# One power on GpSimd for the inverse norms, and reciprocals of one column in thirty-two

## The chip, the cores and the metric

The kernel runs on one core of a Trainium2 chip. The metric is the device time of one execution in microseconds (us). A core has TensorE (PE, the products), VectorE (DVE), ScalarE (ACT), GpSimd (POOL) and queues that start transfers (DMA); the queue used for nearly all of them is that of SyncE (SP). Each engine carries out its instructions in the order in which the program lists them and waits, where needed, for others.

## The reference

The inputs `q`, `k` and `v` have 8 batches, 12 heads, 448 rows and 64 columns; all numbers are float32 on arrival.

```
rmsnorm(x, g) = x / sqrt(mean(x * x) + 1e-6) * g          # over the 64 columns
q_n, k_n = rmsnorm(q, g_q), rmsnorm(k, g_k)
scores = q_n @ k_n^T / sqrt(64)
attn = exp(scores - max) / (sum of exp over the keys + 1e-9)
x = (attn @ v), heads side by side: 3584 rows x 768 columns
out = (silu(x @ w_gate) * (x @ w_val)) @ w_out             # 768 -> 1536 -> 768
```

The two places that matter here are the inverse root of the norms (one number for each row of `q` and of `k`) and the division by the sums over the keys (one number for each query).

## The kernel before

The function `fast` does all the work; `general` is there for gains outside a range and isn't run with these inputs. The heads are handled in pairs: 48 pairs, `m = 0 .. 47`, each handled by a call of `attention(m)`. The rows of the matrices after the attention are handled in four blocks of two batches, `block(n)`. Every product with a weight matrix is made of 15 products of combined thirds (the lists `UP_ORDER` and `DOWN_ORDER`), with sums of the operands formed beforehand (`sides` for the activations, `convert` for the weights) and sums of the results afterwards (`read`).

Nothing is issued in the order in which the Python functions are called. Each step calls `order.add(engine, us, when, emit, ...)` with a planned duration `us`, a due time `when`, the steps that it follows and the buffers that it takes or uses. At the end `order.run()` walks through all steps, picks the next for each engine by planned times, and calls the `emit` functions in that order. So a new planned duration changes the order of instructions on all engines. Two modes of ACT, `logarithms` and `silu`, have their own table loads (lines L552 and L1402 of the profile); a step that names the other mode makes a load.

The profile falls into an **opening** of some 140 us, in which the first twelve pairs are prepared and weighted while the first of the 18 pieces of weights are loaded, converted and stored again in device memory, and four blocks. In a block the up products (L1328) run first, then the down products (L1502) together with the attention of twelve later pairs.

One pair goes through these steps:

- SP loads `q` and `k` into tiles named `qk`, within `work` in the profile (L728), and `v` (L744, L747).
- ACT squares both (L754); DVE adds up each run of 32 columns (L768); ACT swaps halves between partitions with four small copies (L778); DVE adds the two halves (L782). The result `ss` has 28 columns on 128 partitions.
- `inverse_root`: on ACT a logarithm (L678) and an exponential (L679) give an estimate `rr`; on DVE three instructions (L684, L685, L686) improve it by one Newton step.
- GpSimd scales `k` and `q` by `rr` (L795), DVE transposes them in 32-by-32 squares (L811), ACT scales the queries by the gains (L814).
- PE makes the scores (L840, four parts), ACT the exponentials (L855). In the opening PE adds these up over the keys (L947 with four terms); later GpSimd (L860) and DVE (L866) add most of them first.
- PE makes the weighted values (L916); ACT copies one half of the result (L1005) and DVE adds the other (L1008).
- `invert`, on DVE: the reciprocal of the sums, 224 columns (L982). The tile of sums has four strips of 32 partitions, and within a strip all 32 rows hold the same numbers, as each strip is a product with a constant matrix (`many`, `halves`).
- The reciprocals are spread to 128 partitions, in the opening by a product (L990) and later by eight copies on ACT (L1000), and DVE multiplies (L1012).

GpSimd also makes the sums of weight thirds in `convert` (L1199, L1202), ahead of which come two ACT copies (L1146, L1150) and six DVE steps (L1168, L1174, L1180). The loads of pieces that go into the places ES, PAIRS and the third of GT wait for the last sum over keys of the opening.

The rings of buffers that the change touches are `ss=2`, `rr=4`, `rd=1` (reciprocals) and the `t=2` tiles of squares and scaled values.

Of the kernel before, what the change touches and what calls it, by code (L numbers as in the profile page):

```python
# [9 lines left out]
F32 = mybir.dt.float32  # L10
U32 = mybir.dt.uint32
I64 = mybir.dt.int64
AF = mybir.ActivationFunctionType
ALU = mybir.AluOpType
# [346 lines left out]
class Order:  # L361
# [24 lines left out]
    def add(  # L386
        self, engine, us, when, emit, after=(), takes=(), uses=(), port=False, kb=0, group=None,
        mode=None, early=None, rank=0.0, slack=0.1,
    ):
        piece = dict(  # L390
            engine=engine, us=us, when=when, emit=emit, takes=takes, port=port, kb=kb,
            group=group, mode=mode, early=early, rank=rank, slack=slack,
            after=[a for a in after if a is not None], end=None, n=len(self.pieces),
        )
        for tile_of in (*takes, *uses):
            self.users.setdefault(tile_of, []).append(piece)
        self.pieces.append(piece)
        return piece
# [79 lines left out]
def fast(  # L478
# [41 lines left out]
    nc = tc.nc  # L520
    B, H, S, D = q.shape
    DM = H * D
    DFF = moe_w_gate.shape[1]
    P = 128
    NJ = 4
    Q = S // 2
# [6 lines left out]
    C = 32  # L533
# [6 lines left out]
    const = ctx.enter_context(tc.tile_pool(name="const", bufs=1))  # L540
# [3 lines left out]
    ctx.enter_context(tc.manual_schedule())  # L544

    BUFS = dict(
        qk=4, v=2, t=2, QT=2, KT=2, e=4, ea=7, eh=2, sums=1, inv=1, rd=1, rows=3, st=2, at=2, ss=2,
        rr=4, ws=2, **{x + str(i): 1 for x in "vw" for i in range(6)},
    )

# [3 lines left out]
    order = Order(BUFS, dict(logarithms=load_tables))  # L554
    tiles = {}
# [10 lines left out]
    def take(name, key, shape):  # L566
        if name in ("e", "ea"):
            at = order.turn[name] % BUFS[name]
            tiles[name, key] = es[:, at] if at < BUFS["e"] else more_es[:, at - BUFS["e"]]
            return tiles[name, key]  # L570
        if name in OFTEN:
            at = OFTEN[name] + order.turn[name] % BUFS[name]
            tiles[name, key] = spare[:, ts(at, S)]
            return tiles[name, key]
        if name == "eh":
            at = order.turn["eh"] % BUFS["eh"]
            tiles[name, key] = more[:, at].rearrange("p (h q) -> p h q", h=2)
            return tiles[name, key]
        if name in WORK:
            at, size = WORK[name]  # L580
            at += order.turn[name] % BUFS[name] * size
            n = 1
            for length in shape[1:]:
                n *= length
            x = work[0 : shape[0], at : at + n]
            letters = "abcd"[: len(shape) - 1]
            x = x.rearrange(
                f"p ({' '.join(letters)}) -> p {' '.join(letters)}",
                **dict(zip(letters, shape[1:])),
            )  # L590
            tiles[name, key] = x
            return x
        pool = psum if name in ("st", "at") else sbuf
        tiles[name, key] = pool.tile(shape, F32, name=name, bufs=BUFS[name])
        return tiles[name, key]
# [33 lines left out]
    gq2 = const.tile([P, 1], F32, name="gq2")  # L629
    gk2 = const.tile([P, 1], F32, name="gk2")  # L630
    gg = const.tile([P, 1], F32, name="gg")

# [29 lines left out]
    down_products = {}  # L664


    GAIN = 2.0**24

    SCALE = 2.0**8
    SPREAD = 6.0  # L670

    def inverse_root(m, sums, of, when, rank=0.0):


        def estimate():
            ss = of()
            rr = take("rr", m, list(ss.shape))
            nc.scalar.activation(rr, ss, AF.Ln, scale=GAIN**-2)  # L678
            nc.scalar.activation(rr, rr, AF.Exp, scale=-0.5)  # L679

        def improve():
            ss, rr = of(), tiles["rr", m]
            times = nc.vector.scalar_tensor_tensor
            times(ss, rr, GAIN**-2, ss, op0=ALU.mult, op1=ALU.mult)  # L684
            times(ss, ss, -0.5, rr, op0=ALU.mult, op1=ALU.mult)  # L685
            times(rr, ss, 1.5, rr, op0=ALU.add, op1=ALU.mult)  # L686

        first = order.add(
            "ACT", 0.5, when, estimate, after=[sums], uses=[("ss", m)], takes=[("rr", m)],
            mode="logarithms", rank=rank,  # L690
        )
        return order.add(
            "DVE", 0.45, when + 1.0, improve, after=[first], uses=[("ss", m), ("rr", m)],
            rank=rank,
        )

    NC = S // C
    clusters = {}
# [4 lines left out]
    def attention(m):  # L703
# [7 lines left out]
        b, c = batch_pair(m)  # L711
        base, span = pair_time(m)

        ready = base - span
        early = m < EARLY
        rank = 60.0 if early else 0.0
# [40 lines left out]
        for x in range(2):  # L757
# [3 lines left out]
                    after=[loaded[x], *squares], uses=[("qk", (m, x))] + [("t", m)] * x,  # L761
# [26 lines left out]
        )  # L788
        sums = add("ACT", 0.9, ready - 16.0, swap, after=[sums], uses=[("ss", m)])
        sums = add("DVE", 0.15, ready - 15.0, both, after=[sums], uses=[("ss", m)])  # L790
        rr = inverse_root(m, sums, lambda: tiles["ss", m][:, 0], ready - 14.0, rank)

        def scale(x):
            rr = tiles["rr", m][:, ts(x, NC)].rearrange("p (c one) -> p c one", one=1)
# [184 lines left out]


        def invert():
            nc.vector.reciprocal(take("rd", m, [P, Q]), tiles[den])  # L982


        def spread_place():
# [24 lines left out]
        def divide():  # L1010
# [5 lines left out]
        )  # L1016
        joined = add("DVE", 0.64, when + 4.0, join, after=[copied, last], uses=at[1:])
        inv = add(
            "DVE", 1.52, when + 4.0, invert, after=[all_sums], uses=[] if of_bank else [den],
            takes=[("rd", m)],  # L1020
        )
        if early:
            inv = add(
# [565 lines left out]


    nc.gpsimd.memset(many, SCALE)
    nc.gpsimd.memset(halves, 0.0)
    for x in range(2):
        nc.gpsimd.memset(halves[ds(D * x, D), x], SCALE)
# [7 lines left out]
    for i in range(P // C):  # L1602
# [2 lines left out]
    gains = order.add(  # L1605
        "DVE", 0.2, 9.0,
        lambda: nc.vector.scalar_tensor_tensor(
            out=gg, in0=gq2, scalar=8.0 * GAIN**-2, in1=gk2, op0=ALU.mult, op1=ALU.mult
        ),
        early=0.0,  # L1610
    )
# [21 lines left out]
@with_exitstack  # L1633
def kernel(
    ctx: ExitStack,
    tc: tile.TileContext,
    q: bass.AP,
    k: bass.AP,
    v: bass.AP,
    g_q: bass.AP,  # L1640
    g_k: bass.AP,
    moe_w_gate: bass.AP,
    moe_w_val: bass.AP,
    moe_w_out: bass.AP,
    out: bass.AP,
):


    nc = tc.nc
    args = (q, k, v, g_q, g_k, moe_w_gate, moe_w_val, moe_w_out, out)  # L1650
    D = q.shape[3]
    guard = ctx.enter_context(tc.tile_pool(name="guard", bufs=1))
    g2 = guard.tile([1, 2, D], F32, name="g2")
    gp = guard.tile([1, D], F32, name="gp")
    top = guard.tile([1, 1], F32, name="top")
    fits = guard.tile([1, 1], mybir.dt.int32, name="fits")
    for i, x in enumerate((g_q, g_k)):
        nc.scalar.dma_start(g2[:, i], x.rearrange("(one d) -> one d", one=1))
    nc.vector.tensor_tensor(out=gp, in0=g2[:, 0], in1=g2[:, 1], op=ALU.mult)
    nc.vector.tensor_reduce(  # L1660
        out=top, in_=gp, axis=AX.X, op=ALU.max, apply_absolute_value=True
    )
    nc.vector.tensor_scalar(out=fits, in0=top, scalar1=8.0, scalar2=None, op0=ALU.is_le)
    fast(tc, *args)
    fits = nc.values_load(fits[0:1, 0:1], min_val=0, max_val=1)
    with tc.If(fits == 0):
        general(tc, *args)
# [30 lines left out]
```

## Time and profile before

| what | value |
|---|---|
| median of 3 runs | 1487.9 us (1486.89 to 1488.19) |
| span of the profiled execution, first to last instruction | 1484.0 us |
| distance of the median from that span | 3.9 us |
| PE busy, mean granted clock | 1425.0 us, 0.997 |
| DVE, ACT, POOL busy | 916.0, 681.5, 414.1 us |
| PE idle ahead of its first product | 14.66 us |

The page gives no time of the profiled execution other than its span; what lies around it can only be seen as the distance from the median of the runs. A row of a group in the profile reads: line, engine, operation, output and inputs by the program's names, shapes and count, then busy time in us and the mean in ns of one instruction, then the idle time of that engine just ahead of them and what ended most of it. A row of a wait reads: the engine and group that waited, what it waited for, the total in us, how many times, and the longest.

### The profile page before, as it was taken

How to read it: one execution, taken by the hardware profiler on the slowest of the kernel's cores; microseconds unless marked ns; L12 is line 12 of the kernel's file. 1: busy time of each engine (PE TensorE's matmuls, PEld its weight loads, DVE VectorE, ACT ScalarE, POOL GpSimd, SP SyncE). 2: the span in 40 equal slices, each digit the busy share in tenths (PEclk: the TensorE clock that was granted, in tenths of full speed). 3: DMA queues.
4: the chain of work that ended last, by engine and by line, in shares of the span. 5: the costliest groups of instructions: out<-in, count | busy, mean ns of one | idle time of the engine just before them, and what ended most of it. 6: DMA issues, size and time to landing. Idle time of an engine off the chain costs nothing.

```text
span 1484.0 us, 19470 instructions
## 1 busy us (share of the span) xinstructions
PE 1425.0 (96%) x6672; PEld 675.4 (46%) x6672; DVE 916.0 (62%) x1405; ACT 681.5 (46%) x1366; POOL 414.1 (28%) x468
## 2 busy tenths in 40 slices
PE   5789999999999999999999999999999999999998
PEld 2334544443444455544444445554444445555553
DVE  4777887877978544355886733454786854432533
ACT  6774544437775322445767422354676532122100
POOL 2454586636444100012544200011343410000000
PEclk9999999999999999999999999999999999999999
DMA  7767999974453432533344432352353442222235
GB/s 165 158 144 236 292 308 341 296 219 90 99 115 85 113 106 71 138 103 90 74 111 110 100 117 73 106 136 77 96 119 85 90 119 89 80 98 73 83 98 107
DMA packets 415921, 193.30 MB, mean 130 GB/s; under 512 B 324164, under 2 KB 397892, under 8 KB 409668
## 3 DMA queue, kind: packets, MB, share of 16 engines
q1 hardware_dynamic: 402688, 190.35, 48.0%
q10 hardware_dynamic: 12996, 1.61, 0.7%
q8 instruction: 55, 0.90, 0.3%
q14 instruction: 54, 0.44, 0.1%
q0 software_dynamic: 128, 0.00, 0.0%
HBM read 157.29 MB, written 34.60 MB: 129 GB/s over the span
## 4 chain that ended last, share of the span: by engine, by line
PE 73%; DVE 3%; ACT 2%; issue 1%; DMA 1%; SPq 1%; ACTq 0%; DVEq 0%
PE mm L1502 22%; PE mm L1328 20%; PE at L1328 20%; PE st L840 6%; PE at L916 5%; PE st L947 1%; ACT spare L1000 1%; ACT es L855 1%; DVE rd L982 1%; DMA out_dram<-spare 0%; SPq L728 0%; DVE ss L782 0%; DMA work<-in_k_dram 0%; DVE ss L768 0%; DVE sums L866 0%
## 5 line engine op out<-in xcount | busy, mean ns | idle before, releaser
L1328 PE MATMUL mm<-xs,ws 128*128 128x448 f32 x960 | 401.2, 540 | 4.4 <-DVE spare L1276 2.2
L1328 PE MATMUL at<-xs,ws 128*128 128x448 f32 x960 | 400.6, 540 | 4.1 <-DVE v L1274 2.6
L1328 PEld LDWEIGHTS mm<-xs,ws 128*128 128x128 f32 x960 | 181.5, 190 | 185.8 <-issue 173.8
L1328 PEld LDWEIGHTS at<-xs,ws 128*128 128x128 f32 x960 | 181.9, 190 | 184.6 <-issue 172.6
L795 POOL TENSOR_TENSOR work<-work,rr 128x448 f32<-128x448 f32 x96 | 105.9, 1122 | 503.5 <-DVE rr L686 245.2
L840 PE MATMUL st<-work 64*64 64x448 f32 (+1 forms) x1536 | 155.1, 508 | 27.3 <-ACT work L814 21.2
L1502 PE MATMUL mm<-gt,ws 128*128 128x448 f32 x448 | 177.2, 545 | 0.0
L1272 DVE TENSOR_TENSOR gt<-gt,mm 128x448 f32<-128x448 f32 x64 | 39.7, 621 | 185.1 <-PE mm L1328 171.3
L1502 PE MATMUL mm<-hs,ws 128*128 128x448 f32 x384 | 152.1, 545 | 0.9 <-DVE ss L684 0.9
L855 ACT ACTIVATE es<-st 128x896 f32<-128x896 f32 x129 | 114.3, 913 | 56.1 <-PE at L916 42.8
L860 POOL TENSOR_TENSOR sums<-es 128x896 f32<-128x896 f32 x36 | 75.7, 2104 | 195.8 <-PE st L947 83.2
L1402 ACT ACTIVATE st<-gt 128x448 f32<-128x448 f32 x96 | 52.4, 547 | 163.8 <-DVE gt L1276 85.9
L1000 ACT COPY spare<-rd 32x224 f32<-32x224 f32 x288 | 108.1, 375 | 35.0 <-DVE rd L982 30.7
L1502 PEld LDWEIGHTS mm<-gt,ws 128*128 128x128 f32 x448 | 82.9, 190 | 84.2 <-issue 81.0
L916 PE MATMUL at<-es,v 64*64 64x448 f32 x1032 | 110.2, 545 | 7.2 <-ACT xs L1005 3.3
L1270 ACT COPY gt<-mm 128x448 f32<-128x448 f32 x80 | 42.5, 531 | 141.5 <-PE mm L1328 141.4
L1502 PEld LDWEIGHTS mm<-hs,ws 128*128 128x128 f32 x384 | 71.1, 190 | 72.9 <-issue 70.9
L840 PEld LDWEIGHTS st<-work 64*64 64x64 f32 x1536 | 50.9, 134 | 108.7 <-issue 38.1
L1270 ACT COPY v<-at 128x448 f32<-128x448 f32 x96 | 51.1, 532 | 83.2 <-PE at L1328 80.0
L860 POOL TENSOR_TENSOR sums<-sums,es 128x896 f32<-128x896 f32 x36 | 78.7, 2187 | 2.8
L811 DVE STREAM_TRANSPOSE work<-work 128x448 f32<-128x448 f32 x96 | 59.2, 627 | 25.2 <-POOL work L795 23.1
L916 PEld LDWEIGHTS at<-es,v 64*64 64x64 f32 x1032 | 39.7, 134 | 67.4 <-issue 57.4
(150 smaller groups left out, 1568.7 us busy)
## 6 DMA issues: line engine op xcount, KB each, us to landing
ws<-up_sides SPq DMA_DIRECT2D x32, 1024.0 KB, 4.9
ws<-down_sides SPq DMA_DIRECT2D x16, 1024.0 KB, 5.0
ws<-down_sides SPq DMA_DIRECT2D x28, 512.0 KB, 4.0
ws<-up_sides SPq DMA_DIRECT2D x16, 768.0 KB, 4.6
work<-in_q_dram SPq DMA_DIRECT2D x192, 56.0 KB, 2.4
work<-in_k_dram SPq DMA_DIRECT2D x188, 56.0 KB, 2.5
out_dram<-spare SPq DMA_DIRECT2D x168, 56.0 KB, 1.9
v<-in_v_dram SPq DMA_DIRECT2D x96, 96.0 KB, 2.5
```

The costliest lines, as they stand in the source:

```text
L795: nc.gpsimd.tensor_tensor(out=tiles["t", m][:, x], in0=tiles["qk", (m, x)], in1=rr.to_broadcast([P, NC, C]), op=ALU.mult,)
L811: nc.vector.transpose(to, tiles["t", m][:, x].rearrange("p c f -> p (c f)"))
L840: nc.tensor.matmul(st[ds(D * x, D), h, 0:n], tiles["KT", m][rows, ds(P * j + D * of_keys, D)], tiles["QT", m][rows, ds(Q * of_queries, n)] ...
L855: nc.scalar.activation(e, tiles["st", (m, j)][:, :, 0 : S * width(j) // P], AF.Exp)
L860: nc.gpsimd.tensor_tensor(out=to, in0=tiles["e", (m, 0)] if j == 1 else to, in1=e, op=ALU.add)
L916: nc.tensor.matmul(tiles["at", (m, x)][ds(D * h, D), queries], tiles["v", m][rows, j, h], tiles["e", (m, j)][rows, h], start=j == 0, stop= ...
L1000: nc.scalar.copy(inv[ds(D * h + C * to, C), ts(x, Q)], tiles["rd", m][ds(D * h + C * x, C)])
L1270: nc.scalar.copy(to, ps)
L1272: nc.vector.tensor_tensor(out=to, in0=old, in1=ps, op=ALU.add)
L1328: nc.tensor.matmul(ps(), w[:, at, which, c], xs[:, SLOT[x], c], start=fresh and c == 0, stop=c == NC2 - 1, skip_group_check=True,)
L1402: nc.scalar.activation(take(*act, [P, 2, TB])[:, 0, 0:S], to, AF.Silu)
L1502: nc.tensor.matmul(banks[s][:, 0:S], w[:, at, s, g], where[x][:, g], start=fresh and g == 0, stop=g == NG - 1, skip_group_check=True,)
```

## The change

The inverse root becomes one GpSimd instruction, a power of `ss` to a tile that holds -0.5, planned at 0.5 us; the function `inverse_root` and its two steps on ACT and DVE are gone, and with them the constant `GAIN` that kept the logarithm in range. The reciprocal of the sums is taken on one column out of each 32: a transpose of the 32-by-32 squares brings 32 different queries under each other, 7 columns are inverted, and a second transpose of these, each repeated 32 times, gives back the layout of before. It is planned at 0.95 us for 1.52, and takes one further small tile, `rc`.

```diff
-        qk=4, v=2, t=2, QT=2, KT=2, e=4, ea=7, eh=2, sums=1, inv=1, rd=1, rows=3, st=2, at=2, ss=2,
+        qk=4, v=2, t=2, QT=2, KT=2, e=4, ea=7, eh=2, sums=1, inv=1, rd=1, rc=1, rows=3, st=2, at=2, ss=2,
...
+    minus_half = const.tile([P, 1], F32, name="minus_half")
...
-    GAIN = 2.0**24
-
...
-    def inverse_root(m, sums, of, when, rank=0.0):
-
-
-        def estimate():
-            ss = of()
-            rr = take("rr", m, list(ss.shape))
-            nc.scalar.activation(rr, ss, AF.Ln, scale=GAIN**-2)
-            nc.scalar.activation(rr, rr, AF.Exp, scale=-0.5)
-
-        def improve():
-            ss, rr = of(), tiles["rr", m]
-            times = nc.vector.scalar_tensor_tensor
-            times(ss, rr, GAIN**-2, ss, op0=ALU.mult, op1=ALU.mult)
-            times(ss, ss, -0.5, rr, op0=ALU.mult, op1=ALU.mult)
-            times(rr, ss, 1.5, rr, op0=ALU.add, op1=ALU.mult)
-
-        first = order.add(
-            "ACT", 0.5, when, estimate, after=[sums], uses=[("ss", m)], takes=[("rr", m)],
-            mode="logarithms", rank=rank,
-        )
-        return order.add(
-            "DVE", 0.45, when + 1.0, improve, after=[first], uses=[("ss", m), ("rr", m)],
-            rank=rank,
-        )
...
-        rr = inverse_root(m, sums, lambda: tiles["ss", m][:, 0], ready - 14.0, rank)
+
+        def roots():
+            nc.gpsimd.tensor_tensor(
+                out=take("rr", m, [P, 2 * NC]), in0=tiles["ss", m][:, 0],
+                in1=minus_half.to_broadcast([P, 2 * NC]), op=ALU.pow,
+            )
+
+        rr = add(
+            "POOL", 0.5, ready - 14.0, roots, after=[sums], uses=[("ss", m)], takes=[("rr", m)]
+        )
...
         def invert():
-            nc.vector.reciprocal(take("rd", m, [P, Q]), tiles[den])
+            rd, rc = take("rd", m, [P, Q]), take("rc", m, [P, Q // C])
+            nc.vector.transpose(rd, tiles[den])
+            nc.vector.reciprocal(rc, rd.rearrange("p (c i) -> p c i", i=C)[:, :, 0])
+            every = rc.rearrange("p (c one) -> p c one", one=1).to_broadcast([P, Q // C, C])
+            nc.vector.transpose(rd, every)
...
         inv = add(
-            "DVE", 1.52, when + 4.0, invert, after=[all_sums], uses=[] if of_bank else [den],
-            takes=[("rd", m)],
+            "DVE", 0.95, when + 4.0, invert, after=[all_sums], uses=[] if of_bank else [den],
+            takes=[("rd", m), ("rc", m)],
         )
...
     nc.gpsimd.memset(many, SCALE)
+    nc.gpsimd.memset(minus_half, -0.5)
...
-            out=gg, in0=gq2, scalar=8.0 * GAIN**-2, in1=gk2, op0=ALU.mult, op1=ALU.mult
+            out=gg, in0=gq2, scalar=8.0, in1=gk2, op0=ALU.mult, op1=ALU.mult
...
-    gp = guard.tile([1, D], F32, name="gp")
+    gp = g2[:, 0]
```

## The prediction

> **What bounds the kernel now.** I read the totals first, then the slices, the list of what TensorE (PE) waited for, the stretches of the first 140 us, the chain that ended last, and last the groups that the edit touches.
>
> ```profile
> PE 1425.0 (96%) x6672; PEld 675.4 (46%) x6672; DVE 916.0 (62%) x1405; ACT 681.5 (46%) x1366; POOL 414.1 (28%) x468
> ...
> PE   5789999999999999999999999999999999999998
> ```
>
> PE is busy for 1425.0 of 1484.0 us and no product is removed, so an edit on the other engines can only win some of the 59.0 us in which PE stands still, or the gaps between its groups. Where those lie is in the table by stretches (PE, weight loads, DVE, ACT and POOL busy, clock, DMA share, GB/s):
>
> ```profile
> 0.00:20.00 20.00, 5.34 (x40) 1.98 (x40) 7.47 (x23) 9.18 (x22) 6.56 (x16) 1.00 0.76 146
> 20.00:40.00 20.00, 15.95 (x198) 7.05 (x191) 13.87 (x24) 17.67 (x33) 4.29 (x4) 1.00 0.77 180
> 40.00:60.00 20.00, 14.28 (x181) 5.95 (x179) 13.93 (x27) 13.78 (x28) 7.30 (x12) 1.00 0.68 167
> 60.00:80.00 20.00, 16.30 (x172) 6.83 (x168) 17.73 (x29) 16.77 (x33) 13.79 (x21) 1.00 0.81 190
> 80.00:100.00 20.00, 15.78 (x174) 7.42 (x175) 17.67 (x28) 14.13 (x29) 13.05 (x19) 0.94 0.67 133
> ```
>
> The seven stretches up to 140 us hold 105.6 us of PE work. The first product starts at 14.66 us, so 19.8 us are lost between it and 140 us: the opening, in which twelve pairs of heads are prepared while the weights are converted. No engine is full there, but DVE and ACT reach 17.7 of 20. Of the other idle time 14.7 us lie ahead of the first product, 7.4 in the last stretch, and 17.1 in the 1260 us between, so the blocks are full. The waits by releaser say who keeps PE:
>
> ```profile
> PE st L840 <- ACT work L814: 21.2, 6, 14.7
> PE at L916 <- ACT xs L1005: 3.3, 2, 2.3
> PE st L840 <- ACT es L855: 3.1, 11, 0.4
> PE at L916 <- DVE xs L1008: 2.7, 2, 2.1
> ...
> PE mm L990 <- DVE rd L982: 2.0, 2, 1.3
> PE st L840 <- DVE rd L982: 1.3, 2, 1.1
> ```
>
> ACT is the last releaser almost everywhere (of the 21.2 us, 14.7 are the start), then DVE. The timeline of the opening shows thirteen gaps over 0.6 us, 17.8 us in all; it also shows two of the longest (2.10 us at 44.4, 2.58 at 58.3) behind an ACT square that stood until a load of keys landed, so not every gap is a matter of busy engines.
>
> **What the Trainium skill says.** "VectorE: DVE Perf Modes", section on the hardware budget: a reciprocal repeats its divide step eight times. The trace agrees in kind: 1552 ns for 224 columns, where other DVE work takes about 1 ns a column. "GPSIMD Engine Reference", section 7: a dependent fp32 chain costs 4 cycles an element and step; no page prices a power, and no such instruction is in this trace. "PSUM — Partial Sum Buffer" says that ACT, DVE and GpSimd queues are strictly first in, first out; the trace agrees at 43.7 us, where a scaling whose input was there since 40.6 stood behind that square. "ScalarE: Activation LUTs", on the table load: about 1283 ns each, as here (1283).
>
> **The change, part by part.** Durations from these rows:
>
> ```profile
> L982 DVE RECIPROCAL rd<-st 128x224 f32<-128x224 f32 x37 | 57.4, 1552 | 3.9 <-PE st L947 3.8
> ...
> L684 DVE SCALAR_TENSOR_TENSOR ss<-rr,ss 128x28 f32<-128x28 f32 x48 | 12.0, 250 | 15.1 <-ACT rr L679 14.9
> ...
> L679 ACT ACTIVATE rr<-rr 128x28 f32<-128x28 f32 x48 | 10.9, 226 | 1.5
> L686 DVE SCALAR_TENSOR_TENSOR rr<-ss,rr 128x28 f32<-128x28 f32 x48 | 10.8, 224 | 1.7
> ```
>
> 1. Inverse root. Per pair ACT loses two instructions (L678 224 ns, L679 226: 0.45 us) and DVE three (L684 250, L685 187, L686 224: 0.66 us); GpSimd gets one power of 128x28. Times 48: ACT -21.6 us, DVE -31.7.
> 2. The power's price, d. From below: the plain GpSimd sums of 128 and 256 columns (L1199) take about 0.46 and 0.73 us, 2.1 ns a column, so 28 columns cost 0.26 us if a power is as cheap as a sum. From above: if it is a chain of some 30 dependent steps (my assumption; a logarithm and an exponential of about 15 each), the page's 4 cycles give 120 cycles an element, 28 x 120 at the page's 1.2 GHz = 2.8 us, 3.1 with the start. I take 1.0 us, nearer the lower end, as 16 lanes work on independent numbers. Total +48 us, between +12 and +149, on an engine 28% busy.
> 3. The chain to GpSimd's scaling. Now from the end of the sum (L782) to the start of L795: 1.40 us for pair 0 (9.99 to 11.39), 1.80 for pair 1, 2.36 for the fourth. After: about 0.2 us of hand-over and d, 1.2 us. Shorter by 0.2 to 1.2 a pair; up to d of about 1.6 it isn't longer. In the compiled order each power stands directly ahead of its pair's two scalings, and what is queued behind it are the conversion sums (L1199, L1202), which stood behind the scalings before: the new wait of GpSimd for DVE's sum replaces its wait for DVE's root at the same place. The start gains 0.2: nothing, to be safe; dear, it costs d - 1.2 once.
> 4. Reciprocals. A transpose of 224 columns: 448 cost 627 ns (L811) and a 28-column DVE row 224, so 0.96 ns a column, 0.41 us. Two of them, and a reciprocal of 7 columns: a start of 0.16 (the one-column L1607) and 7 x 6.2 ns = 0.20. Together 1.02 against 1.55: -0.53 a pair, x48 = -25.6. Bounds: nothing gained if transposes from PSUM or of a broadcast cost 0.25 more each; -0.75 if they run at the reciprocal's start plus 0.55 ns a column.
> 5. Tables. The compiled order has 8 loads of each set for 11: 6 x 1.28 = 7.7 us of ACT, in the blocks, where PE does not wait for them.
> 6. The planner re-orders all engines with the new costs. Runs of full-array products on PE fall from 69 to 63; the chain shows 8 such products at 3.20 us, 16 at 6.21 and 24 at 9.23, so 3.01 for eight and 0.2 for each run begun. 6 x 0.2 = 1.2 us saved. DMA counts are equal on every queue; in the opening SP's second load of value weights moves behind one more pair's loads. Memset, one shorter gain product, the shared guard tile: outside any wait, covered by the 5 us in which the first loads land.
>
> In sum DVE loses 57 us (14.3 in the opening), ACT 29 (5.4 there). In the blocks this is worth almost nothing: PE work covers it. What shows there: a 1.12 us wait on the reciprocal at 359 us loses 0.5, and one of 0.92 us put down to L684 at 333 us perhaps the same: 1.0.
>
> In the opening a gap can shrink by what its releaser loses per pair: ACT 0.45, DVE 1.19. Twelve pairs by 0.45 is 5.4 us, by 1.19 it is 14.3, and all gaps are 17.8. Two gaps (4.7 us) hang on loads. I take 5.0, just under ACT's share, as ACT releases most. It reaches the end only if block 0 follows: its later weights are loaded after the last sum over keys of the opening (SP stood 9.0 us on it), so that chain moves along, but DMA is at 0.8 to 1.06 up to 300 us; I give back 1.0.
>
> Sum: -5.0 - 1.2 - 1.0 + 1.0 = **-6.2 us**. Against the profiled execution: span 1484.0 to 1477.8. The page gives no other time of that execution; the median of the runs, 1487.9, lies 3.9 above its span, and I keep that distance: 1481.7.
>
> **Rivals.**
> A. *The power is dear* (slower). Place: POOL between the sum and the scalings of the opening's pairs. For: no row prices it, one instruction does the work of five, and the queue is in order. Against: the chain has 1.4 to 2.4 us to give. PE's gaps behind L814 and the start are five places where a longer chain shows: 5 x (d - 1.6) against 6.2 gained, so it decides from d = 2.8 us, near my upper price. At d = 5: +17.0 - 6.2 = +10.8, 1498.7; POOL would hold 54 + 60 us of the first 120, so nearly full. Above 5.5 us POOL bounds the opening, and it grows by 12 us for each further us.
> B. *Hidden anyway* (same). The gaps hang on loads of q and k and on buffers, and block 0 on its weights: then only the runs of products and the two waits in the blocks remain, -2.2: 1485.7. For: the two gaps on loads, DMA shares of 0.67 to 0.81. Against: most waits name ACT and DVE.
> C. *A worse order.* The new PE order puts all scores of pair 1 ahead of the first weighted product and two weighted pairs in a row; if an in-order wait of 1 us comes at six of the twelve pairs, the opening loses 6 instead of winning 5, and -2.2 stays: +3.8, 1491.7. It turns slower from three such waits. For: a plan made for half a us of power meets another d. Against: fewer changes of kind on PE.
> D. *All gaps close*: -15, 1473. DVE's share would allow it; the loads speak against it.
> That the edit doesn't do what it says is excluded by the compiled order: 48 powers, 96 transposes, 48 small reciprocals, the old rows gone.
>
> **How the numbers follow.** A measurement of this kernel can tell about 0.2%, 3 us, from no change. Forecast 0.46 (1477 to 1486; 0.03 of it within 0.2%), D 0.08, B 0.19, C 0.12, A 0.15. Faster: 0.43 of the forecast, D's 0.08 and, as B lies 2.2 below, 0.04 of B: 0.55. Same: the other 0.15 of B and the forecast's 0.03: 0.18. Slower: A and C: 0.27. The range reaches from D's 1473 to 1499, A at d = 5: about 0.04 lies below and 0.1 above. The forecast's own range is 1477 to 1486.
>
> **What would show it.** Right: no L678 to L686; a GpSimd row of 48 near 1 us; two transposes near 0.41 and a reciprocal near 0.20; DVE about 859 us, ACT 652; PE idle between its first product and the start of block 0 about 15 instead of 19.8 us; block 0 earlier by about 5. Wrong: a power over 2.8 us and waits of L811 on POOL (A); the same gaps on loads (B); new waits of L916 or L840 in the first 60 us (C). A saving inside the blocks beyond 2 us would mean that PE was not full there.

## The result and the profile after

The changed kernel takes **1597.5 us** (median of 4 runs, 1596.4 to 1600.5) against 1487.4 us of the kernel before on the same chip (1486.3 to 1488.2): a ratio of 1.0747, interval [1.0732, 1.0762]. It is 110 us slower, where 1481.7 us was predicted and 1499 was the top of the range. The profiled execution spans 1594.3 us against 1484.0.

The page of the changed kernel first: its totals, the clock in 40 slices, and the group of the powers.

```profile
PE 1461.1 (92%) x6672; PEld 686.7 (43%) x6672; DVE 864.4 (54%) x1357; ACT 655.5 (41%) x1264; POOL 641.8 (40%) x517
...
PEclk9888999998999999999998999999999999999999
...
L767 POOL TENSOR_TENSOR rr<-ss,minus_half 128x28 f32<-128x28 f32 x48 | 238.6, 4971 | 436.4 <-DVE ss L756 413.8
```

DVE and ACT fell about as forecast (864 and 656 us; 859 and 652 were said). The power is the surprise: 4971 ns on the mean, 1.0 us in the prediction. And PE, which has the same 6672 products, is busy for 36 us more: the mean granted clock fell from 0.997 to 0.969. What PE waited for, the three largest entries:

```profile
PE st L823 <- ACT work L797: 58.9, 12, 18.5
PE st L823 <- ACT es L838: 34.2, 24, 9.0
PE at L899 <- DVE xs L995: 8.4, 3, 5.4
```

The first line is the old one (it was L814 and 21.2 us): scores wait for the scaled queries. The second was 3.1 us. No entry of PE's list names POOL. GpSimd is two steps back, on DVE's and ACT's own lists of waits:

```profile
DVE work L794 <- POOL work L778: 178.2, 58, 6.8
```

```profile
ACT work L797 <- DVE work L794: 122.8, 27, 8.0
```

Both were about 20 us before (23.1 and 18.9). To see where the time goes, split each profile at the first product with up weights (L1315, the end of the opening) and at the same point of each block, and part each stretch into PE's busy and idle time. PE does the same number of products in each stretch of each kernel (about 1197 in the opening, 1590 in block 0), so more busy time is a slower clock or shorter runs of products. The two answers for the opening and block 0, of after and of before (PE busy is the second number, the clock the third from the end):

```profile
0.00:168.90 168.90, 116.00 (x1196) 50.18 (x1197) 85.54 (x160) 88.75 (x157) 123.77 (x115) 0.91 0.59 139
168.90:579.70 410.80, 368.93 (x1590) 169.04 (x1589) 285.28 (x425) 197.69 (x362) 255.62 (x283) 0.96 0.64 179
```

```profile
0.00:140.10 140.10, 105.66 (x1196) 46.91 (x1197) 100.18 (x174) 92.79 (x181) 66.61 (x107) 0.99 0.72 168
140.10:505.10 365.00, 353.29 (x1591) 163.04 (x1589) 292.85 (x434) 200.93 (x386) 193.59 (x266) 1.00 0.72 201
```

The opening lost 28.8 us (18.5 idle, 10.3 busy), block 0 45.8 (30.2 idle, 15.6 busy), blocks 1 and 2 17.8 and 18.0 (about 13 idle and 5 busy each), block 3, which has no pairs left to prepare, nothing. **So 81 of the 110 us are in the blocks, of which the prediction had said that PE work covers what happens on the other engines.** A piece of block 1 shows how. The timeline of the changed kernel, for GpSimd, DVE, ACT and PE in turn (start, duration, engine, in brackets the wait just before it):

```profile
843.73 5.11 POOL L767 TENSOR_TENSOR rr<-ss,minus_half 128x28 f32<-128x28 f32 x1 [6.87 <-DMA v<-in_v_dram]
...
851.97 2.34 POOL L843 TENSOR_TENSOR sums<-sums,es 128x896 f32<-128x896 f32 x1
...
857.17 4.79 POOL L767 TENSOR_TENSOR rr<-ss,minus_half 128x28 f32<-128x28 f32 x1 [1.96 <-DVE ss L756]
862.05 1.84 POOL L778 TENSOR_TENSOR work<-work,rr 128x448 f32<-128x448 f32 x2
```

```profile
854.35 2.00 DVE L849 TENSOR_TENSOR sums<-sums,more 64x448 f32<-64x448 f32 x2 [1.97 <-POOL sums L843]
...
856.92 0.17 DVE L756 SCALAR_TENSOR_TENSOR ss<-ss 128x28 f32<-128x28 f32 x1
...
863.92 1.17 DVE L794 STREAM_TRANSPOSE work<-work 128x448 f32<-128x448 f32 x2 [5.76 <-POOL work L778]
```

```profile
864.66 0.67 ACT L797 ACTIVATE work<-work,gg 128x448 f32<-128x448 f32 x1 [6.30 <-DVE work L794]
865.23 1.70 ACT L838 ACTIVATE es<-st 128x896 f32<-128x896 f32 x2
```

```profile
866.18 1.82 PE L823 MATMUL st<-work 64*64 64x224 f32 x10 [9.02 <-ACT es L838]
```

Read it from the end. PE stands 9.02 us for an exponential (L838). That exponential stood in ACT's queue behind L797, the scaled queries of a later pair, which waited 6.30 us for transposes that waited for GpSimd's second power. That power in turn came late because the sums over keys (L843) had stood behind the first one on GpSimd, DVE's L849 waited for them, and L756, which releases the power, stood behind L849. Two powers in one chain, of 5.11 and 4.79 us, each planned at 0.5: 8.9 us more than planned, and PE's gap is 9.02.

### The profile page after: what moved, and what is told of

The parts are those of the page before. It is cut to its first block, busy times and chain, and to the rows that moved or that the text cites. A ratio compares the mean times of both kernels' runs of the same rounds, so it can differ in the third digit from the quotient of the medians.

```text
span 1594.3 us, 19399 instructions
## 1 busy us (share of the span) xinstructions
PE 1461.1 (92%) x6672; PEld 686.7 (43%) x6672; DVE 864.4 (54%) x1357; ACT 655.5 (41%) x1264; POOL 641.8 (40%) x517
## 4 chain that ended last, share of the span: by engine, by line
PE 59%; issue 7%; DVE 7%; POOL 4%; ACT 3%; DMA 3%; SPq 1%; POOLq 0%; DVEq 0%; ACTq 0%
PE at L1315 18%; PE mm L1315 18%; PE mm L1489 14%; PE st L823 4%; PE at L899 3%; ACT spare L987 2%; POOL sums L843 2%; DVE xs L1040 2%; DMA v<-in_v_dram 1%; POOL work L778 1%; DVE sums L849 1%; DVE xs L999 1%; PE st L930 1%; ACT es L838 1%; DMA work<-in_k_dram 1%
## 5 line engine op out<-in xcount | busy, mean ns | idle before, releaser
L767 POOL TENSOR_TENSOR rr<-ss,minus_half 128x28 f32<-128x28 f32 x48 | 238.6, 4971 | 436.4 <-DVE ss L756 413.8
L1315 PE MATMUL mm<-xs,ws 128*128 128x448 f32 x960 | 401.2, 540 | 6.4 <-DVE spare L1263 2.2
L1315 PE MATMUL at<-xs,ws 128*128 128x448 f32 x960 | 400.8, 540 | 4.8 <-DVE v L1259 2.6
L823 PE MATMUL st<-work 64*64 64x448 f32 (+1 forms) x1536 | 174.0, 557 | 97.7 <-ACT work L797 58.9
L1315 PEld LDWEIGHTS mm<-xs,ws 128*128 128x128 f32 x960 | 181.5, 190 | 188.2 <-issue 173.3
L1315 PEld LDWEIGHTS at<-xs,ws 128*128 128x128 f32 x960 | 181.6, 190 | 185.6 <-issue 171.0
L1489 PE MATMUL mm<-gt,ws 128*128 128x448 f32 x448 | 182.0, 558 | 0.0
L838 ACT ACTIVATE es<-st 128x896 f32<-128x896 f32 x129 | 114.4, 914 | 68.8 <-PE at L899 46.5
L823 PEld LDWEIGHTS st<-work 64*64 64x64 f32 x1536 | 54.2, 143 | 186.7 <-ACT work L797 67.0
L843 POOL TENSOR_TENSOR sums<-es 128x896 f32<-128x896 f32 x36 | 75.0, 2083 | 141.0 <-ACT xs L992 52.3
L987 ACT COPY spare<-rd 32x224 f32<-32x224 f32 x288 | 108.1, 375 | 49.7 <-DVE rd L969 43.4
L778 POOL TENSOR_TENSOR work<-work,rr 128x448 f32<-128x448 f32 x96 | 90.4, 960 | 3.6
L797 ACT ACTIVATE work<-work,gg 128x448 f32<-128x448 f32 x48 | 32.0, 667 | 130.1 <-DVE work L794 122.8
```

What stands on the lines that cost most here:

```text
L767: nc.gpsimd.tensor_tensor(out=take("rr", m, [P, 2 * NC]), in0=tiles["ss", m][:, 0], in1=minus_half.to_broadcast([P, 2 * NC]), op=ALU.pow,)
L778: nc.gpsimd.tensor_tensor(out=tiles["t", m][:, x], in0=tiles["qk", (m, x)], in1=rr.to_broadcast([P, NC, C]), op=ALU.mult,)
L823: nc.tensor.matmul(st[ds(D * x, D), h, 0:n], tiles["KT", m][rows, ds(P * j + D * of_keys, D)], tiles["QT", m][rows, ds(Q * of_queries, n)] ...
L838: nc.scalar.activation(e, tiles["st", (m, j)][:, :, 0 : S * width(j) // P], AF.Exp)
L843: nc.gpsimd.tensor_tensor(out=to, in0=tiles["e", (m, 0)] if j == 1 else to, in1=e, op=ALU.add)
L987: nc.scalar.copy(inv[ds(D * h + C * to, C), ts(x, Q)], tiles["rd", m][ds(D * h + C * x, C)])
```

## The experiments

Names: e1 to e14. "The planner" is the list of planned durations from which `order.run()` makes the order. Stage times (us) from the profiled execution of each kernel; opening and block 0 as PE busy + idle:

| kernel | median | opening | block 0 | block 1 | block 2 |
|---|---|---|---|---|---|
| before | 1487 | 140.1 = 105.7 + 34.4 | 365.0 = 353.3 + 11.7 | 350.2 | 350.4 |
| after | 1597.5 | 168.9 = 116.0 + 52.9 | 410.8 = 368.9 + 41.9 | 368.0 | 368.4 |
| e1 | 1498.2 | 147.8 = 114.0 + 33.8 | 376.4 = 357.8 + 18.6 | 347.8 | 347.8 |
| e2 | 1597.4 | 164.5 = 115.5 + 49.0 | 420.7 = 372.6 + 48.1 | 367.4 | 365.9 |
| e3 | 1488.7 | 144.5 = 111.6 + 32.9 | 368.4 = 354.5 + 13.9 | 347.8 | 347.8 |
| e4 | 1516.8 | 169.3 = 109.4 + 59.9 | 366.8 = 357.4 + 9.4 | 350.7 | 350.4 |
| e5 | 1485.4 | 142.1 = 110.2 + 31.9 | 365.5 = 354.3 + 11.2 | 349.8 | 349.9 |
| e6 | 1483.2 | 138.7 = 105.2 + 33.5 | 365.9 = 353.6 + 12.3 | 347.9 | 347.8 |
| e7 | 1504.0 | 145.8 = 111.0 + 34.8 | 380.8 = 359.3 + 21.5 | 348.7 | 348.7 |
| e9 | 1526.1 | 149.4 = 110.9 + 38.5 | 386.4 = 361.3 + 25.1 | 354.8 | 354.8 |
| e10 | 1499.0 | 140.2 = 106.0 + 34.2 | 375.0 = 358.3 + 16.7 | 352.5 | 352.5 |
| e11 | 1505.9 | 146.3 = 110.7 + 35.6 | 378.5 = 360.7 + 17.8 | 350.4 | 350.5 |
| e12 | 1489.8 | 142.6 = 109.5 + 33.1 | 373.1 = 357.9 + 15.2 | 348.8 | 348.7 |
| e13 | 1509.5 | 161.2 = 111.7 + 49.5 | 368.8 = 358.1 + 10.7 | 350.4 | 350.7 |
| e14 | 1484.1 | 133.0 = 103.2 + 29.8 | 374.3 = 356.6 + 17.7 | 347.8 | 347.8 |

Executions of the kernel before lie between 1483.5 and 1490.6 us over all runs, and the stages are those of one execution each (that of e12 is 3.5 us above its median, that of e6 2.9 below). e8, whose order is that of the kernel before up to its last GpSimd instructions, gives a second execution of it: 141.7 = 108.1 + 33.6, 364.6, 350.3, 350.4. So one or two microseconds of the opening or of block 0 are not to be read, while blocks 1 and 2 repeat within 0.1.

**e1, the reciprocals alone.** The kernel before with the new reciprocals, that is, the changed kernel with `inverse_root` as before:

```diff
-        rr = add("POOL", 0.5, ready - 14.0, roots, ...)
+        rr = inverse_root(m, sums, lambda: tiles["ss", m][:, 0], ready - 14.0, rank)
```

> The kernel before with the reciprocals between two transposes alone; the root stays on ScalarE and VectorE, and the planner is told 0.95 us for the reciprocals. Theory L (the length of the power makes the whole loss): 1480 to 1488, as VectorE loses 0.53 to 0.57 us a pair and nothing is added on GpSimd. Rival O (the new order of instructions makes most of the loss): over 1500, as this edit re-orders the engines too.

Measured: 1498.2, ratio 1.0075 [1.0061, 1.0090]. That is between the two theories: slower by 11 us, though its instructions are shorter. Half of the change makes the kernel slower.

**e2, the power alone.** The kernel before with the power; `invert` and its planned 1.52 us untouched.

> The changed kernel with the old reciprocals of 224 columns; the power stays. Theory L: 1590 to 1605, as the power's 4.8 us are still in each pair's chain. Rival O: anywhere between 1490 and 1600; well under 1560 if the transposes have a share in the loss.

Measured: 1597.4, ratio 1.0742 [1.0725, 1.0760], in theory L's range. The whole loss comes with the power; the reciprocals add nothing to it.

**e3, the power made short.** The changed kernel with

```diff
-                in1=minus_half.to_broadcast([P, 2 * NC]), op=ALU.pow,
+                in1=minus_half.to_broadcast([P, 2 * NC]), op=ALU.mult,
-    nc.gpsimd.memset(minus_half, -0.5)
+    nc.gpsimd.memset(minus_half, 1.0 / 512)
```

> The changed kernel with a product by 1/512 in place of the power: the inverse root is left out (the rows are scaled by their norms instead), with the same instruction count, order, shapes and plan; an instruction of about 0.3 us instead of 4.8. Theory L: 1478 to 1486, about what was predicted with a power of 1.0 us. Rival O: over 1550, since order and waits are those of the changed kernel.

Measured: 1488.7, ratio 1.0012 [1.0003, 1.0021]. The order is that of the changed kernel; only the time of the 48 instructions is gone (375 ns each), and 109 us with it. DVE's and ACT's own work is nearly the same (busy 859 us for 864 and 658 for 656), so the power costs by what waits for it, not by slowing these two. But theory L's range, up to 1486, is missed by 3 us: the forecast's gain doesn't appear. e5 to e7 and e14 look for it.

**e4, the planner told the truth.** The changed kernel with one number changed:

```diff
-            "POOL", 0.5, ready - 14.0, roots, after=[sums], uses=[("ss", m)], takes=[("rr", m)]
+            "POOL", 4.85, ready - 14.0, roots, after=[sums], uses=[("ss", m)], takes=[("rr", m)]
```

> The changed kernel with the planner told 4.85 us for the power instead of 0.5, so that it orders all engines around its true length. Theory L: 1560 to 1600, since the power still holds GpSimd for 4.8 us a pair and lies in each pair's chain. Rival M (it is the misplanned order, as TensorE, ScalarE and GpSimd queue in order behind a result that comes 4.3 us later than planned): 1490 to 1530.

Measured: 1516.8, ratio 1.0200 [1.0183, 1.0217], in rival M's range. **The same instructions in another order are 81 us faster.** Blocks 1 and 2 are back at 350, block 0 at 367. What is left is in the opening. The list of PE's waits of e4 has a new entry:

```profile
PE mm L1315 <- DMA ws<-up_sides: 19.4, 1, 19.4
```

GpSimd also forms the sums of the weights (L1186, L1189), and the powers push them back. In e4 it starts its last power of the opening at 128.4 us. Then it makes the pair's scalings and conversion sums, with one pause of 0.21 us, until after 169, the point at which PE's wait ends.

**e5, e6, e7, e12: reciprocal and plan taken apart.** Each number is the planned duration of `invert`; the inverse root is as before in all four.

```diff
e5, e6: new reciprocal;  e7, e12: old reciprocal
 inv = add(
-    "DVE", 1.52, when + 4.0, invert, ...
+    "DVE", 1.52,                          # e5: the order of before
+    "DVE", 0.95,                          # e7: the order of e1
+    "DVE", 1.52 if early else 0.95,       # e6, e12: early = the pairs of the opening
```

> The reciprocals between two transposes, the inverse root as before, and the planner still told 1.52 us for the reciprocal, so that the instructions stand in exactly the order of the kernel before on every engine. Theory O (the loss of e1, +11 us, is the new order that the new duration gives the planner, and the transposes themselves save time): 1483 to 1487.5, since DVE is freed by about 25 us and nothing else moves. Rival T (the transposes themselves, in PSUM reads or in rounding of the queues, cost what the order seemed to): 1495 or more, as e1.

> The reciprocals between two transposes, the inverse root as before, the planner told 1.52 us in the opening and 0.95 us in the blocks. Theory O: the opening keeps the order of before (140 us to the first up product, or a little less) and block 0 too, blocks 1 and 2 win the 2.5 us each that e1 and e3 showed: 1480 to 1484, faster than before. Rival: the loss of e1 in block 0 (376.4 against 364.9) comes from the blocks' own order, not from a late opening: 1488 to 1495.

> The kernel before with one number changed: the planner is told 0.95 us for the reciprocal of 1.55 us, so that the instructions stand in the order of e1 with the old reciprocal. Theory O: the loss of e1 is all here, and more, since DVE is not freed: 1498 to 1505. Rival T: 1486 to 1490, as before.

> The kernel before with only the planner's number changed, 0.95 in the blocks and 1.52 in the opening, the reciprocal itself as before. It parts e6's gain (-3.5 us) into order and work. From e7, whose blocks 1 and 2 took 348.7 against 350.3 of before and 347.8 of e1: about 3 of 5 us are the order. Expected 1484 to 1487; if the saved DVE work is what counts, as before (1487) or up to 1 us more.

Measured: e5 1485.4, ratio 0.9989 [0.9981, 0.9996]; e6 1483.2, 0.9978 [0.9971, 0.9985]; e7 1504.0, 1.0115 [1.0099, 1.0132]; e12 1489.8, 1.0019 [1.0012, 1.0026]. Theory O stands: the transposes do no harm (e5), and e1's loss is in the order (e7, which has the order of e1 and no transposes, loses more). At one order the new reciprocal gains each time: 5.8 us from e7 to e1, 6.6 from e12 to e6, 1.4 from before to e5. e12 missed its expectation by 3 us: in an order made for short reciprocals, long ones cost more. In the profiled executions block 0 takes 7 us more than in e6; the medians differ by 6.6 in all. e6 is the fastest version found that does all of the work, 0.2% faster than the kernel before.

The table also says how e1's order costs time in the opening. From before to e1 PE's idle time did not grow (34.4, 33.8); its busy time did, by 8.3 us. e1 has fewer but longer gaps (3.27, 3.54 and 4.65 us are the longest; before, after the first product, none over 2.6), and its mean clock over the opening is 0.92 for 0.99. So in this execution e1's opening loses by the clock alone. Part of the 8.3 us may be chance: e8 and e5, in the order of before, have 108.1 and 110.2 us. But over whole executions all six of e1 have a clock of 0.988 to 0.991, and all of the kernel before 0.993 to 0.998. That the longer gaps bring the lower clock is likely, not shown.

**e8, the power's price.** Ten instructions at the end of GpSimd's queue:

```diff
+    for n in (1, 7, 14, 28, 56):
+        for op in (ALU.pow, ALU.mult):
+            nc.gpsimd.tensor_tensor(out=root[:, 0:n], in0=base[:, 0:n], in1=power[:, 0:n], op=op)
```

> The kernel before with ten instructions at the end of GpSimd's queue: a power and a product, each of 128 partitions by 1, 7, 14, 28 and 56 columns, on constants. Theory F (the power's time is a price per element): 28 columns take 4.8 us as in the changed kernel, 14 about 2.4, 56 about 9.6, 1 below 0.4. Rival: a fixed cost of some 3 to 4 us for entering the function, then little a column: 1 column takes over 3 us. Base 64 and exponent -0.5 throughout; if the time hangs on the values, 28 columns will not take 4.8.

Measured, durations in the timeline: the power takes 0.84, 1.88, 2.84, 5.23 and 9.54 us for 1, 7, 14, 28 and 56 columns, the product 0.19 to 0.36. From 28 to 56 columns that is 0.154 us a column, with some 0.7 to 0.9 us ahead of it. Theory F stands in the main: the time grows with the columns. One column takes twice its 0.4, so a smaller fixed part is there too.

**e9, e10: a power of half the width.**

```diff
-                in1=minus_half.to_broadcast([P, 2 * NC]), op=ALU.pow,
+            for x, op in ((1, ALU.pow), (0, ALU.mult)):   # 14 columns each
-            "POOL", 0.5, ready - 14.0, roots, ...
+            "POOL", 3.1, ready - 14.0, roots, ...         # e10 only
```

> The changed kernel with the power on 14 of the 28 columns (the keys); the queries' 14 are only multiplied by 1/512, so their inverse root is left out. From e8, 2.84 us for the power and 0.22 for the product: d is 3.1 where it was 4.8, and the planner is still told 0.5, so the order is that of the changed kernel and of e3. If the loss grows in proportion to what the plan leaves out (0 at about 0.3, +109 at 4.8), the run takes about 1555. If the gaps have slack first (theory of break-even, the prediction's 1.6 to 2.8), less than half the loss: under 1535, and blocks 1 and 2 at most 5 us over e3's 347.8.

> e9 with the planner told 3.1 us for the two instructions; again the queries' inverse root is left out. Theory C (GpSimd's capacity in the opening: its queue also holds the conversions of the weights, and at d = 4.85 these land late): at 3.1 GpSimd has some 21 us more room in the opening than in e4, most of the 29 us are gone, the first up product starts at 142 to 150, 1487 to 1496. Rival H (the longer chain from the sums to the scaling costs PE a gap for each pair): the loss is in proportion, some 18 us, first up product near 158, about 1504. Blocks 1 and 2 within 1 us of 350 in both.

Measured: e9 1526.1, ratio 1.0263 [1.0247, 1.0279]; e10 1499.0, 1.0075 [1.0060, 1.0091]. The loss is not in proportion: from 0.4 to 3.2 us for the root (the two instructions take 2766 and 428 ns in e9) it grows by 37 us, from there to 5.0 by 71. That is the case with slack first, though blocks 1 and 2 are 7.0 over e3, where at most 5 was expected. With the length planned, the opening is back at 140.2, as theory C has it, but the total missed C's range by 3 us: block 0 is 10 us longer than before, and blocks 1 and 2 are 2.3 and 2.1 longer, where at most 1 was expected.

**e11, the power only after the opening.** e4 with

```diff
+        if early:
+            rr = inverse_root(m, sums, lambda: tiles["ss", m][:, 0], ready - 14.0, rank)
+        else:
             rr = add("POOL", 4.85, ready - 14.0, roots, ...)
```

> e4 (the planner told 4.85 us for the power) with the inverse root of before on the twelve pairs of the opening, the power on the other 36; the reciprocals between transposes everywhere, planned at 0.95. Theory C: the opening loses only what e1's and e7's order loses there (first up product at 140 to 148), block 0 between 365 and 376, blocks 1 and 2 at 350 as in e4: 1486 to 1498. Rival: the power also costs beside full blocks, even where the planner knows its length: over 1502.

Measured: 1505.9, ratio 1.0122 [1.0107, 1.0138], above theory C's range and in its rival's. The opening is C's, 146.3 against 169.3 of e4: it is the opening's own powers that make it late. The sum of opening and block 0 is that of e1 (524.8 and 524.2), and blocks 1 and 2 come out at 350.4 where e1 has 347.8. So the rival was partly right: beside full blocks a power that the planner knows takes away the 2.6 us a block that e1 wins there.

**e13, e14: the two still open.** e4 and e3, each with the reciprocal planned as in e6.

```diff
-            "DVE", 0.95, when + 4.0, invert, ...
+            "DVE", 1.52 if early else 0.95, when + 4.0, invert, ...
```

> e4 (the planner told 4.85 us for the power) with the reciprocal planned at 1.52 us in the opening and 0.95 in the blocks, as in e6. Theory C (GpSimd has to do 12 powers of 4.8 us in the opening beside the conversions of the weights, and those land late): the order of the reciprocals matters little, first up product at 160 or later, 1508 to 1518. Rival (the 29 us of e4 are mainly the order that e1 and e7 showed, 19 us to the end of block 0): first up product near 150, 1495 to 1502.

> The changed kernel with a product by 1/512 in place of the power (the inverse root is left out) and the reciprocal planned at 1.52 us in the opening and 0.95 in the blocks: the prediction's own case, a cheap instruction on GpSimd in place of five, in an order that e6 showed to be good. The prediction's step for the opening (5 us from ACT's and DVE's freed time): first up product at 134 to 136, 1476 to 1480. If the opening hangs on loads and on buffers: 138 to 140 as e6, 1482 to 1485.

Measured: e13 1509.5, ratio 1.0141 [1.0126, 1.0157]; e14 1484.1, 0.9978 [0.9970, 0.9986]. In e13 theory C's forecast holds: PE still waits 12.57 us for converted weights at the end of the opening. GpSimd's timeline of e13 around its last power of the opening, a few rows of a stretch of 45 us that holds only these two pauses:

```profile
127.83 4.80 POOL L767 TENSOR_TENSOR rr<-ss,minus_half 128x28 f32<-128x28 f32 x1 [0.26 <-DVE ss L756]
132.71 1.84 POOL L778 TENSOR_TENSOR work<-work,rr 128x448 f32<-128x448 f32 x2
134.51 2.49 POOL L1189 TENSOR_TENSOR gt<-gt 128x128 f32<-128x128 f32 x4
...
158.51 2.08 POOL L1189 TENSOR_TENSOR es<-es 128x256 f32<-128x256 f32 x3 [1.00 <-DVE es L1167]
```

```profile
161.17 3.32 PE L1315 MATMUL mm<-xs,ws 128*128 128x448 f32 x4 [12.57 <-DMA ws<-up_sides]
```

Not all of that wait need be GpSimd's. SP stood for its sums (14.3 us between 100 and 172 us), but the last store that these weights follow had landed at 146.54, and their load was issued at 154.45, behind fifteen other loads in SP's queue, and landed at 161.04. In the kernel before the load went out as soon as the store had landed (125.39 and 125.32). How much of the 12.57 us each of the two makes was not parted.

In the kernel before GpSimd had time to wait there (its first rows of the conversion of `spare`):

```profile
126.83 0.72 POOL L1202 TENSOR_TENSOR hs<-hs 128x128 f32<-128x128 f32 x1
134.25 2.06 POOL L1202 TENSOR_TENSOR spare<-spare 128x256 f32<-128x256 f32 x3 [6.71 <-DVE spare L1180]
```

e14 is the prediction's own case, a short instruction in place of five, in a good order. Its opening is 7.1 us shorter, more than forecast; block 0 is 9.3 longer, and the total lies in the other range, 1482 to 1485. The stretches of e14, and the place in block 0:

```profile
0.00:133.00 133.00, 103.22 (x1197) 46.34 (x1198) 83.47 (x155) 88.76 (x157) 59.50 (x100) 1.00 0.70 160
133.00:507.30 374.30, 356.59 (x1589) 166.39 (x1587) 280.27 (x430) 198.27 (x362) 207.77 (x298) 0.98 0.72 203
```

```profile
190.22 3.33 PE L1315 MATMUL mm<-xs,ws 128*128 128x448 f32 x4 [5.12 <-DMA ws<-up_sides]
...
336.46 2.52 PE L823 MATMUL st<-work 64*64 64x224 f32 x16 [5.17 <-ACT work L797]
```

PE came to the weights sooner, and they landed no sooner: 5.12 us are handed back in one wait, which ends at 190.22 (in the kernel before PE waited 0.55 us for the same piece, until 187.65). Another 5.17 us are a wait for a pair's scaled queries, whose cause was not followed. What e14 gains in the end lies in blocks 1 and 2, 2.4 and 2.6 us, as in e6.

**The sum of the loss**, in medians: before to e6 (the reciprocals, planned by stage) -4; e6 to e13 (the power in place of the root, its length planned) +26; e13 to e4 (the reciprocals' plan in the opening) +7; e4 to the changed kernel (the power planned at a tenth of its length) +81; together 110. This +81 is another figure than the 81 us that the blocks lose, though it lies nearly all there: e4's opening is as long as the changed kernel's.

## Why the prediction was wrong

The forecast named the right quantity, d, and the right rival, A; it fell on the terms below. The price by itself is the smaller part: in an order planned for it the kernel is 22 us slower than before (e13). The rest of the 110 us is the plan's.

1. **Step 2, the power's price.** 1.0 us was taken and 3.1 called the most; it takes 4.97 us on the mean, and 0.154 us a column in e8. With the figures of the Trainium skill's "GPSIMD Engine Reference" that the step used (4 cycles from section 7, 1.2 GHz from section 1), 0.154 us would be 185 cycles or, as an estimate, some 46 dependent steps. No run shows the steps. The 30 of the prediction were an assumption without a row behind it, and nothing made them an upper bound.
2. **"In the blocks ... PE work covers it", and rival A's place, the opening alone.** This is the largest miss: it was said of what the blocks could win, and nothing was put there for what they could lose. 81 of 110 us lie in them. In-order queues carried GpSimd's lateness through DVE to ACT and into an exponential that PE needed (the 9.02 us above). The prediction saw that what stands behind the power are the conversion sums, and priced them at nothing; in the blocks sums over keys (L843) stand there, which it did not name.
3. **The plan's 0.5 us.** Step 6 and rival C spoke of the new order only as a source of small waits. The planner arranges all engines for its numbers, so what a wrong one leaves out comes back as waits on the others: 81 us (e4 against the changed kernel). Even the reciprocals' new number, which is about right, costs 11 us by the order that it makes (e1), and 17 with the old reciprocal (e7), where rival C had the opening lose 6.
4. **Rival A's size.** 10.8 us at d = 5. Its start was right: the first product moved from 14.66 to 18.49 us, 3.8, where d - 1.2 = 3.6 was said. Its limit, "above 5.5 us POOL bounds the opening", was too high: with the plan right, 3.2 us leave the opening at 140.2 (e10), and with 4.9 PE already waits 12.6 us for the weights (e13; part of that may be SP's order).
5. **The clock** was in no step. PE's busy time grew by 36 us, a third of the loss. The traces mark stretches at half clock; half of PE's busy time in them is 33.9 us in the changed kernel and 1.7 in the one before, so the clock makes about 32 of the 36. The Trainium skill's "TensorE: Matmul & The Clock Gate", section "HAM oscillation — how this bites in real kernels", says that pauses of more than about 3.4 us let the clock be halved, and that each return is paid for. The traces agree in kind, but not in the limit: in the kernel before no gap after the first product is over 2.6 us, and yet its clock is 0.94 from 80 to 100 us. Around the 9.02 us gap of the changed kernel:

```profile
850.00:860.00 10.00, 7.16 (x56) 2.88 (x54) 6.12 (x9) 1.52 (x5) 7.96 (x4) 1.00 0.05 8
860.00:870.00 10.00, 3.82 (x25) 1.22 (x26) 2.06 (x4) 4.27 (x7) 3.97 (x4) 0.50 0.77 187
870.00:880.00 10.00, 10.00 (x60) 4.41 (x63) 3.81 (x8) 7.03 (x18) 5.74 (x3) 0.99 0.29 33
```

   The stretch with the end of the gap has a mean clock of 0.50. Block 1, with gaps of 9.02 and 4.00 us, lost 13 us idle and 4.8 by slower products.
6. **The opening's -5.0 and the give-back of +1.0.** In a good order (e14) the first is confirmed and exceeded: -7.1, of which 4.6 is idle time. The second is the term that failed: block 0 gives back 9.3, 5.1 of them in one wait for weights that come no sooner; PE's busy time there is 3.3 longer too. Rival B had the reason of the wait ("block 0 on its weights"). In the order that the changed kernel really has, the opening gains nothing even with a short instruction (e3: idle 1.5 us less, busy 5.9 more, with a mean clock of 0.95).

Steps 1 and 5 were right in kind: ACT lost 26.0 us where 29 was said, DVE 51.6 where 57, and there are 8 table loads of each set for 11. Step 4 was right within 0.02 us. The rows of the changed kernel:

```profile
L969 DVE STREAM_TRANSPOSE rd<-rc 128x224 f32<-128x224 f32 x48 | 19.8, 412 | 1.7
L966 DVE STREAM_TRANSPOSE rd<-st 128x224 f32<-128x224 f32 x37 | 14.8, 399 | 4.5 <-PE st L930 4.3
L967 DVE RECIPROCAL rc<-rd 128x7 f32<-128x7 f32 x48 | 9.7, 201 | 1.6
```

0.40 + 0.20 + 0.41 us against 1.55. "A saving inside the blocks beyond 2 us would mean that PE was not full there", it said: e6 saves 2.3 and 2.6 us in blocks 1 and 2, of which the order alone is 1.4 and 1.7 (e12), so they had a little to give. What separates e11's and e13's 350.5 from e1's 347.8 in the same blocks was not followed to one wait, nor were all of block 0's gaps in the changed kernel; both stay open.

## What to carry to other kernels

An operation that no row of a profile prices must not be bounded by an assumed count of steps. Leave the top open, and work out from which price each stage breaks, in the full stages as well as the loose ones, by following what stands behind it on every in-order queue. Where an order is made from planned durations, a wrong duration is a cost of its own, and the first thing to try is to tell the planner the measured one; a right one can also do harm where the plan was good by accident, so change it stage by stage. Time won ahead of a stage that waits for transfers can come back as a wait for those transfers, as 5.1 of e14's 7.1 us did.

## What the runs showed of the hardware

The power on GpSimd costs 0.15 us for each column of 128 partitions after some 0.7 to 0.9 us; for 28 columns that is more than twenty times a plain product there (5.23 and 0.24 us in e8).

The granted clock is not fixed by the order of instructions. e5 and e6 have the same order throughout the opening, and between 70 and 80 us similar gaps (1.74 and 0.34 us, 1.80 and 0.94). Yet the clock of the profiled execution of e5 fell to 0.70 there, and that of e6 stayed at 1.00:

```profile
70.00:80.00 10.00, 7.91 (x68) 2.95 (x68) 8.26 (x18) 6.49 (x15) 7.39 (x11) 0.70 1.02 263
```

```profile
70.00:80.00 10.00, 7.26 (x96) 3.18 (x88) 8.81 (x19) 8.16 (x17) 7.87 (x11) 1.00 1.04 264
```

Over the whole opening this made 5.0 us of PE's busy time (110.2 and 105.2), out of a spread of 7.7 us between the executions of one kernel (1481.4 to 1489.1 for e5).
